# Adding an expert's scaled outputs into the result by accumulating DMAs instead of GpSimd additions

## The chip, the core and the metric

The kernel runs on one core of one Trainium2 chip. The core has TensorE (PE, matrix products into PSUM), VectorE (DVE), ScalarE (ACT), GpSimd (POOL) and SyncE (SP, which here only issues DMAs), each with its own instruction queue, and 16 DMA engines that serve the queues of SP and POOL. The metric is the device time of one execution in microseconds (us); lower is better.

## The reference

A block-sparse attention gives x, and a mixture of eight experts, all of them applied to every token, gives the result. Cut to what matters here:

```python
x = attn_out.transpose(0, 2, 1, 3).reshape(B * S, H * D)     # 3072 tokens x 512
P = exp(x @ w_gate - max); 8 rounds of row and column normalization   # 3072 x 8
out = np.zeros((N, D), dtype=np.float32)
for e in range(E):                       # E = 8, F = 1024
    h = np.maximum(x @ w1[e], 0.0)
    ye = h @ w2[e]
    out += P[:, e:e + 1] * ye
```

## The kernel before

The first part (some 160 us) computes the attention, expert 0 for all tokens and the routing weights `P_sb`. The rest is experts 1 to 7, and the change is in it alone.

Tokens are taken in three pairs of blocks (`p`, 2 x 512 tokens each). Both products of an expert are done by a Strassen scheme in two-by-two blocks with seven products in place of eight. The first layer works in groups of 4 quads per pair of blocks (`quad`, with `product` at L724): seven products of two 512-column matmuls, evicted by ACT and DVE into a ring of `h` tiles (f16), with DVE's `add_relu` (L764) for two of the four blocks. After every second quad DVE forms four sums of `h` blocks (`h_sum`, L776, 128x1024 f16) that the second layer's products need. Weights get such sums too (`w1_sum` L707, `w2_sum` L717).

The second layer works on 4 columns of tokens per pair of blocks (`pair(e, p, c)`, with `project` at L780): seven products of four 256-column matmuls for two tiles of 128 tokens, `t1` and `t2`. The result is kept as float32 in SBUF, `out_acc` (128 x 24 x 512), and each tile gets its parts like this:

- tile t2: DVE multiplies by P and adds from PSUM (`accumulate`, L808) twice, `z1` and `u3`;
- tile t1, first part: the PSUM tile pY holds its left half after product 1, and its right half's share after product 6 in the same columns. ACT copies it, scaled by P, into the two halves of an SBUF tile `y` (`scaled`, L817: `a1`, `a2`). Product 6 (`p6`) waits for `a1`, product 7 for `a2`. GpSimd then adds `y` into `out_acc` (`add_scaled`, L821: `g1`);
- tile t1, second part, in PSUM tile yps: for even c DVE multiplies and adds (`z2`, L808), after `g1`; for odd c ACT scales it into another `y` tile (`a3`) and GpSimd adds it (`z2`, L821), after `g1`. The very last column (e = 7, p = 2, c = 3) goes as an even one.

There are three `y` buffers. In expert 7 SP stores each tile of `out_acc` once `u3` or `z2` is done (L824).

The order on every engine is fixed when the program is built. A planner (`Plan`) holds all pieces of work as units with an engine, a cost in us, predecessors, a priority and the buffers they open or use; `order()` runs a list schedule with these costs and emits the units as it places them. In the hardware each engine then works through its own queue in that order, waiting for semaphores. A buffer tag listed in the planner's slots is a resource: a unit that opens a buffer can be placed only when all users of the buffer it replaces have been placed, and not before they end. The `y` buffers are not among the tags before the change. A unit on an engine name of its own (such as "LAND") models a delay.

Weights for expert e+1 are loaded by POOL's DMA queue (`load_w1` L189, `load_w2` L195), with a cast from float32 to f16, about an expert ahead. POOL has nothing else to do in this part than these loads and the additions.

Of the kernel before, what the change touches and what calls it, by code (L numbers as in the profile page):

```python
# [9 lines left out]
FP32 = mybir.dt.float32  # L10
# [3 lines left out]
ALU = mybir.AluOpType  # L14
# [19 lines left out]
class Plan:  # L34
# [7 lines left out]
    def add(self, eng, cost, fn, deps=(), prio=0.0, opens=(), uses=(), lag=0.0):  # L42
        u = Unit(eng, cost, fn, [d for d in deps if d is not None], prio, list(opens), lag)
        for b in list(opens) + list(uses):
            b.users.append(u)
        if uses and eng != "PE":
            u.prio -= 100.0
        self.units.append(u)
        return u
# [79 lines left out]
def kernel(  # L129
# [10 lines left out]
    nc = tc.nc  # L140
# [3 lines left out]
    N, DM = out.shape  # L144
    E = moe_w_gate.shape[1]
# [33 lines left out]
    out_acc = persist.tile([128, NT, DM], FP32)  # L179
# [40 lines left out]
    NS = 1  # L220
    NA = 3
    stage = ExitStack()
    with tc.manual_schedule():
# [25 lines left out]
        NPAIR = N // (2 * BLK)  # L249
# [1 line left out]
        HK = KD // 2  # L251
        xs, h_ring = {}, {}

        plan = Plan({"m": 3, "s": NS, "a": NA, "A": 3, "R": 1, "Q": 1})
        add = plan.add

        at, units = {}, {}
# [339 lines left out]
        def keep_busy(n):  # L597

            t = bank("m", "idle")
            for _ in range(n):  # L600
# [6 lines left out]
                          in_=k[0, 0:2].rearrange("j (p g) d -> p j (g d)", g=G))  # L607
        nc.sync.dma_start(out=v_f32.rearrange("p j g d -> p (j g) d"),
                          in_=v[0, 0:2].rearrange("j (g p) d -> p (j g) d", p=128))
# [70 lines left out]
        post = {}  # L680
# [99 lines left out]
        def project(e, p, c, n):  # L780
            if n == 1:
                at["ya", e, p, c] = post["ps"].tile([128, BLK], FP32, tag="A", name="pY", bufs=plan.slots["A"])
            elif n == 5:
                at["z", e, p, c] = bank("m", "yps")
            dst = at["ya" if n in (1, 6, 7) else "z", e, p, c]
            d = slice(HD, DM) if n in (5, 3) else slice(0, HD)
            for f in range(HF):
                lhsT = ring(e, p, f)[:, f % 2, {1: 0, 2: 2, 3: 6, 4: 3, 5: 4, 6: 5, 7: 1}[n], c * 128:(c + 1) * 128]
                rhs = {1: lambda: w2s[e][:, f, 0:HD], 2: lambda: w2s[e][:, HF + f, 0:HD],
                       3: lambda: w2s[e][:, HF + f, HD:DM], 4: lambda: at["t", e, 2][:, f, :],  # L790
                       5: lambda: at["t", e, 0][:, f, :], 6: lambda: at["t", e, 1][:, f, :],
                       7: lambda: w2s[e][:, f, HD:DM]}[n]()
                nc.tensor.matmul(dst[:, d], lhsT=lhsT, rhs=rhs, start=f == 0 and n in (1, 5, 2), stop=f == HF - 1,  # L793
                                 skip_group_check=True)

        def tok(p, c, r):
            return 8 * p + 4 * r + c

        def accumulate(e, p, c, r):

            t = tok(p, c, r % 2)
            o, scalar = out_acc[:, t, :], P_sb[:, t, e:e + 1]
            if r == 3:
                o = o.rearrange("p (i d) -> p i d", i=2)
                y = at["ya", e, p, c][:, None, 0:HD].to_broadcast([128, 2, HD])
            else:
                y = at["z", e, p, c][:]
            nc.vector.scalar_tensor_tensor(out=o, in0=y, scalar=scalar, in1=o, op0=ALU.mult, op1=ALU.add)  # L808

        def scaled(e, p, c, part):  # L810

            t, key = tok(p, c, 0), ("y", e, p, c, part == 2)
            if part != 1:
                at[key] = post["sb"].tile([128, DM], FP32, tag="y", name="y", bufs=3)
            d = (slice(0, HD), slice(HD, DM), slice(0, DM))[part]
            src = at["z", e, p, c][:] if part == 2 else at["ya", e, p, c][:, 0:HD]
            nc.scalar.activation(out=at[key][:, d], in_=src, func=AF.Copy, bias=0.0, scale=P_sb[:, t, e:e + 1])  # L817

        def add_scaled(e, p, c, key):
            o = out_acc[:, tok(p, c, 0), :]  # L820
            nc.gpsimd.tensor_tensor(out=o, in0=o, in1=at.pop(("y", e, p, c, key))[:], op=ALU.add)  # L821

        def store(t):
            nc.sync.dma_start(out=out[t * 128:(t + 1) * 128, :], in_=out_acc[:, t, :])  # L824

        def scale_first(eng, t):
            o, scalar = out_acc[:, t, :], P_sb[:, t, 0:1]
            if eng == "ACT":
                nc.scalar.activation(out=o, in_=o, func=AF.Copy, bias=0.0, scale=scalar)
            else:  # L830
                nc.vector.tensor_scalar_mul(out=o, in0=o, scalar1=scalar)
# [201 lines left out]
        for i in range(PB):  # L1033
# [3 lines left out]

        first = {"T": lambda i: U["tr", i, 0], "Q": lambda i: U["tr", i, 1], "k": lambda i: U["kT", i, 0],
                 "q": lambda i: U["kT", i, 1], "v": lambda i: U["vs", i], "V": lambda i: U["Vs", i],
                 "m": lambda i: U["ks", i], "S": lambda i: U["S", i, 0], "X": lambda i: U["X", i, 0],  # L1040
                 "b": lambda i: U["mk", i, 0], "s": lambda i: U["ss", i, 0], "e": lambda i: U["sx", i, 0],
                 "A": lambda i: U["A", i, 0], "n": lambda i: U["no", i, 0], "t": lambda i: U["xt", i, 0],
                 "x": lambda i: U["x", i, 0]}
# [11 lines left out]
        for i in range(PB, NP):  # L1055
# [3 lines left out]
            if i % PB == PB - 1:  # L1059
                b = i // PB  # L1060
# [111 lines left out]
        def pair(e, p, c):  # L1172
            g = (e - 1) * NPAIR + p
            pr = 2005.0 + 10.0 * (HF * (g + 1) + c)
            ya, z = Buffer("A"), Buffer("m")
            t1, t2 = tok(p, c, 0), tok(p, c, 1)
            first = {t1: [], t2: []}
            if e == 1:
                for t in (t1, t2):
                    u = add({"ACT": 0.75, "DVE": 0.5}, 0, None, [U["P"], U["yo", t]], pr - 20.0)  # L1180
                    u.fn = lambda u=u, t=t: scale_first(u.on, t)
                    first[t] = [u]

            def mul(n, deps, opens=False):
                u = add("PE", 0.44, lambda: project(e, p, c, n), deps + [d for j in range(2) for d in U["D", e, p, j][n]],
                        pr, **{"opens" if opens else "uses": [ya if n in (1, 6, 7) else z]})
                U["Yp", e, p, c, n] = u
                return u

            def ev(eng, us, fn, deps, b):  # L1190
                return add(eng, us, fn, deps + [U["P"]], pr - 5.0, uses=[b])

            T = lambda i: U["w2", e, i]
            p1 = mul(1, [U["w2", e]], True)
            a1 = ev("ACT", 0.46, lambda: scaled(e, p, c, 0), [p1], ya)
            p5 = mul(5, [T(0)], True)
            p4 = mul(4, [T(2), p5])
            z1 = ev("DVE", 0.76, lambda: accumulate(e, p, c, 1), [p4] + first[t2], z)
            p6 = mul(6, [T(1), a1])
            a2 = ev("ACT", 0.46, lambda: scaled(e, p, c, 1), [p6], ya)  # L1200
            g1 = add("POOL", 1.25, lambda: add_scaled(e, p, c, False), [a2] + first[t1])
            p3 = mul(3, [z1])
            p7 = mul(7, [T(3), a2])
            u3 = ev("DVE", 0.76, lambda: accumulate(e, p, c, 3), [p7, z1], ya)
            p2 = mul(2, [p3])
            if c % 2 and (e, p, c) != (E - 1, NPAIR - 1, 3):
                a3 = ev("ACT", 0.68, lambda: scaled(e, p, c, 2), [p2], z)
                z2 = add("POOL", 1.25, lambda: add_scaled(e, p, c, True), [a3, g1])
            else:
                z2 = ev("DVE", 0.76, lambda: accumulate(e, p, c, 0), [p2, g1], z)  # L1210
            U["Y", e, p, c] = z2
            if e == E - 1:
                add("SP", 0.1, lambda: store(t2), [u3])
                add("SP", 0.1, lambda: store(t1), [z2])
# [58 lines left out]
```

## Time and profile before

| what | value |
|---|---|
| median of 3 runs | 708.64 us (707.03 to 708.86) |
| the profiled execution's own time | 706.25 us |
| its span, first to last instruction | 704.4 us |
| PE busy | 667.4 us, 95% |
| DVE busy | 611.2 us, 87% |
| ACT busy | 413.0 us, 59% |
| POOL busy | 264.4 us, 38% |
| granted clock of TensorE | 1.000 |

A row of groups reads: line, engine, operation, written tile<-read tiles, shapes and count, then the group's busy time (us), the mean time of one (ns), and the idle time of the engine just before them with what ended most of it. A row of waits reads: who waited, for whom, us in total, how often, the longest. A row of windows reads: the stretch, its length, then busy time and instruction count of each engine (PE, PE's weight loads, DVE, ACT, POOL where all are listed; PE and its weight loads alone where one line of matmuls is asked for), the granted clock, the DMA engines' busy share and GB/s. A row of the timeline reads: start (us), duration (us), engine, line, operation and tiles, how many were merged, and in brackets the idle time before it with what ended it. Matmuls are pipelined and their ends are modelled, so the time between starts says more than their durations.

### The profile page before, as it was taken

Reading aid. Unit: us, or ns where it says so; the run is one execution under the profiler, and the core shown is the slowest. Engines: PE = TensorE matmul, PEld = TensorE weight load, DVE = VectorE, ACT = ScalarE, POOL = GpSimd, SP = SyncE. Lnnn points to the kernel's source line nnn. Section 1 sums busy time; section 2 is a strip of 40 time slices with the busy share of each in tenths; the row PEclk is TensorE's granted clock in tenths of the full one; section 3 lists DMA queues with packets and bytes.
Section 4 is the critical chain, followed back from the end, with each engine's and each line's share of the span. In section 5 each row is a group of like instructions: output and inputs, shape, how many; then the busy total and the mean of one; then the engine's idle time right before and its main releaser. Section 6 shows DMA issues by size and latency. Waiting matters only on the chain.

```text
span 704.4 us, 13246 instructions
## 1 busy us (share of the span) xinstructions
PE 667.4 (95%) x5130; PEld 434.1 (62%) x5131; DVE 611.2 (87%) x1033; ACT 413.0 (59%) x770; POOL 264.4 (38%) x257
## 2 busy tenths in 40 slices
PE   8999999999999999999999999999999899999996
PEld 4666666546666666665666566565666566565665
DVE  7889877999889987989889987989889988989886
ACT  6677765488655556455655546555554655555652
POOL 8899422001323423234324423324323323233224
PEclk9999999999999999999999999999999999999999
DMA  9999924333003030034003120034003210001224
GB/s 170 173 140 146 144 43 79 67 57 65 0 1 61 7 54 1 1 60 61 0 1 61 19 42 1 1 61 60 1 1 60 30 33 1 1 1 46 90 75 150
DMA packets 95262, 36.43 MB, mean 52 GB/s; under 512 B 76000, under 2 KB 88544, under 8 KB 95200
## 3 DMA queue, kind: packets, MB, share of 16 engines
q0 software_dynamic: 77520, 25.99, 34.4%
q1 hardware_dynamic: 17152, 9.58, 5.7%
q8 instruction: 40, 0.66, 0.4%
q14 instruction: 22, 0.18, 0.1%
q10 hardware_dynamic: 528, 0.02, 0.0%
HBM read 52.45 MB, written 6.29 MB: 83 GB/s over the span
## 4 chain that ended last, share of the span: by engine, by line
PE 58%; DVE 28%; issue 7%; DMA 4%; POOL 2%; SPq 0%; DVEq 0%; POOLq 0%
DVE h L776 13%; PE yps L793 13%; PE pA L742 13%; PE pY L793 10%; PE pQ L742 7%; DVE h L764 5%; PE hps L208 4%; PE yps L213 4%; DVE out_acc L808 4%; PE pR L742 3%; DVE w2sum L717 3%; DMA kT<-kst 1%; DMA w<-in_moe_w_dram 1%; DMA vx<-in_v_dram 1%; DMA Ve<-vx 1%
## 5 line engine op out<-in xcount | busy, mean ns | idle before, releaser
L821 POOL TENSOR_TENSOR out_acc<-out_acc,y 128x512 f32<-128x512 f32 x125 | 173.1, 1385 | 366.3 <-ACT y L817 346.3
L793 PEld LDWEIGHTS <-h 128*128 128x128 f16 x2352 | 228.4, 98 | 105.3 <-DVE h L776 13.9
L817 ACT ACTIVATE y<-pY,P_sb 128x256 f32<-128x256 f32 x168 | 79.9, 476 | 144.6 <-PE pY L793 142.8
L776 DVE TENSOR_TENSOR h<-h 128x1024 f16<-128x1024 f16 x168 | 162.2, 998 | 1.4
L808 DVE SCALAR_TENSOR_TENSOR out_acc<-yps,P_sb,out_acc 128x512 f32<-128x512 f32 x127 | 94.1, 742 | 22.0 <-PE yps L793 21.0
L793 PE MATMUL yps<-w2sum,h 128*128 128x256 f16 x672 | 100.3, 273 | 8.2 <-DVE h L776 8.2
L793 PE MATMUL pY<-w,h 128*128 128x256 f16 x672 | 100.3, 272 | 0.1
L742 PE MATMUL pA<-xT,w 128*128 128x512 f16 x336 | 98.4, 379 | 1.6 <-DVE snap L204 1.6
L793 PE MATMUL yps<-w,h 128*128 128x256 f16 x672 | 93.8, 273 | 1.6 <-DVE out_acc L808 1.4
L742 PEld LDWEIGHTS <-w 128*128 128x128 f16 x672 | 65.7, 98 | 41.0 <-issue 10.5
L742 PEld LDWEIGHTS <-w1sum 128*128 128x128 f16 x504 | 49.3, 98 | 60.3 <-issue 18.9
L808 DVE SCALAR_TENSOR_TENSOR out_acc<-pY,P_sb,out_acc 128x512 f32<-128x512 f32 x84 | 62.5, 744 | 20.3 <-PE pY L793 17.4
L764 DVE CUSTOM_DVE_ANT_0 h<-pA,snap 128x512 f16<-128x512 f32 x84 | 57.2, 680 | 6.1 <-PE pA L742 5.7
L199 ACT ACTIVATE h<-pA 128x512 f16<-128x512 f32 x84 | 50.6, 602 | 19.4 <-PE pA L742 19.2
L764 DVE CUSTOM_DVE_ANT_0 h<-pQ,snap 128x512 f16<-128x512 f32 x84 | 57.4, 683 | 5.0 <-ACT snap L204 2.7
L742 PE MATMUL pQ<-xsum,w1sum 128*128 128x512 f16 x168 | 49.9, 378 | 11.1 <-DVE h L764 11.1
L742 PE MATMUL pA<-xsum,w 128*128 128x512 f16 x168 | 49.9, 379 | 5.4 <-DVE h L764 5.3
L199 ACT ACTIVATE h<-pR 128x512 f16<-128x512 f32 x84 | 50.1, 596 | 6.9 <-PE pR L742 6.8
L793 PE MATMUL pY<-w2sum,h 128*128 128x256 f16 x336 | 51.4, 273 | 0.7
L204 ACT COPY snap<-pQ 128x512 f32<-128x512 f32 x70 | 41.0, 586 | 17.1 <-PE pQ L742 17.1
L742 PE MATMUL pA<-xsum,w1sum 128*128 128x512 f16 x168 | 50.0, 379 | 0.0
L742 PE MATMUL pQ<-xT,w1sum 128*128 128x512 f16 x168 | 50.0, 379 | 0.0
(144 smaller groups left out, 860.2 us busy)
## 6 DMA issues: line engine op xcount, KB each, us to landing
w<-in_moe_w_dram POOLq DMA_DIRECT2D x15, 1024.0 KB, 8.8
out_dram<-out_acc SPq DMA_DIRECT2D x24, 256.0 KB, 2.0
qst<-in_q_dram POOLq DMA_DIRECT2D x32, 96.0 KB, 5.7
vx<-in_v_dram POOLq DMA_DIRECT2D x15, 192.0 KB, 6.9
kst<-in_k_dram POOLq DMA_DIRECT2D x24, 96.0 KB, 6.1
w<-in_moe_w_dram POOLq DMA_DIRECT2D x4, 256.0 KB, 7.1
kst<-in_k_dram POOLq DMA_DIRECT2D x3, 192.0 KB, 4.6
Ve<-vx SPq DMA_DIRECT2D x32, 10.2 KB, 5.4
```

The source lines that it names most:

```text
L199: nc.scalar.activation(out=out, in_=in_, func=AF.Relu, bias=0.0, scale=1.0)
L204: (nc.scalar.copy if eng == "ACT" else nc.vector.tensor_copy)(out=out, in_=in_)
L208: nc.tensor.matmul(hp[:, 0:n], lhsT=w1s[e][:, dk, f * 128:(f + 1) * 128], rhs=xT[:, dk, t0:t0 + n], start=(dk == 0), stop=(dk == KD - 1))
L213: nc.tensor.matmul(yp[:, d], lhsT=h[:, f, c * 128:(c + 1) * 128], rhs=w2s[e][:, f, d], start=(f == 0), stop=(f == KF - 1))
L717: nc.vector.tensor_tensor(out=out_, in0=a, in1=b, op=ALU.subtract)
L742: nc.tensor.matmul(dst[:], lhsT=lhsT, rhs=rhs, start=first and k == 0, stop=k == HK - 1, skip_group_check=True)
L764: nc.vector._custom_dve(dve_ops.TENSOR_ADD_SAT, out=ring(e, p, q)[:, q % 2, blk, :], in0=at[src, e, p, q][:], in1=at.pop(("snap", n, e, p, ...
L776: nc.vector.tensor_tensor(out=h[:, :, out_, :], in0=h[:, :, a, :], in1=h[:, :, b, :], op=op)
L793: nc.tensor.matmul(dst[:, d], lhsT=lhsT, rhs=rhs, start=f == 0 and n in (1, 5, 2), stop=f == HF - 1, skip_group_check=True)
L808: nc.vector.scalar_tensor_tensor(out=o, in0=y, scalar=scalar, in1=o, op0=ALU.mult, op1=ALU.add)
L817: nc.scalar.activation(out=at[key][:, d], in_=src, func=AF.Copy, bias=0.0, scale=P_sb[:, t, e:e + 1])
L821: nc.gpsimd.tensor_tensor(out=o, in0=o, in1=at.pop(("y", e, p, c, key))[:], op=ALU.add)
```

## The change

The two GpSimd additions of `pair` become DMAs from the GpSimd queue that read `y` and add it into `out_acc` in SBUF, in float32. The planner gets a unit for the issue on POOL (1.0 us) and one for the landing (4.0 us); the `y` buffers become a planned resource, and there are four of them. In even columns the DVE part now comes first and the DMA of the first part is issued after it; in odd columns the second DMA waits for the landing of the first. In the last pair of blocks of expert 7 the first part stays an addition on GpSimd and the second is a DVE accumulation in every column.

```diff
-        plan = Plan({"m": 3, "s": NS, "a": NA, "A": 3, "R": 1, "Q": 1})
+        plan = Plan({"m": 3, "s": NS, "a": NA, "A": 3, "R": 1, "Q": 1, "y": 4})
...
-                at[key] = post["sb"].tile([128, DM], FP32, tag="y", name="y", bufs=3)
+                at[key] = post["sb"].tile([128, DM], FP32, tag="y", name="y", bufs=plan.slots["y"])
...
         def add_scaled(e, p, c, key):
             o = out_acc[:, tok(p, c, 0), :]
-            nc.gpsimd.tensor_tensor(out=o, in0=o, in1=at.pop(("y", e, p, c, key))[:], op=ALU.add)
+            nc.gpsimd.dma_start(out=o, in_=at.pop(("y", e, p, c, key))[:], accum_op=ALU.add)
+
+        def add_on_pool(e, p, c):
+            o = out_acc[:, tok(p, c, 0), :]
+            nc.gpsimd.tensor_tensor(out=o, in0=o, in1=at.pop(("y", e, p, c, False))[:], op=ALU.add)
...
+            def landed(part, deps, b):
+                u = add("POOL", 1.0, lambda: add_scaled(e, p, c, part == 2), deps)
+                u = add(f"L{e}.{p}.{c}.{part}", 4.0, None, [u])
+                b.users.append(u)
+                return u
+
+            y1 = Buffer("y")
             p1 = mul(1, [U["w2", e]], True)
             a1 = ev("ACT", 0.46, lambda: scaled(e, p, c, 0), [p1], ya)
+            a1.opens.append(y1)
+            y1.users.append(a1)
...
-            g1 = add("POOL", 1.25, lambda: add_scaled(e, p, c, False), [a2] + first[t1])
...
-            if c % 2 and (e, p, c) != (E - 1, NPAIR - 1, 3):
+            last_pair = (e, p) == (E - 1, NPAIR - 1)
+            if c % 2 and not last_pair:
+                g1 = landed(0, [a2] + first[t1], y1)
                 a3 = ev("ACT", 0.68, lambda: scaled(e, p, c, 2), [p2], z)
-                z2 = add("POOL", 1.25, lambda: add_scaled(e, p, c, True), [a3, g1])
+                y2 = Buffer("y")
+                a3.opens.append(y2)
+                y2.users.append(a3)
+                z2 = landed(2, [a3, g1], y2)
+            elif last_pair:
+                g1 = add("POOL", 1.25, lambda: add_on_pool(e, p, c), [a2] + first[t1])
+                y1.users.append(g1)
+                z2 = ev("DVE", 0.76, lambda: accumulate(e, p, c, 0), [p2, g1], z)
             else:
-                z2 = ev("DVE", 0.76, lambda: accumulate(e, p, c, 0), [p2, g1], z)
+                z2 = ev("DVE", 0.76, lambda: accumulate(e, p, c, 0), [p2] + first[t1], z)
+                z2 = landed(0, [a2, z2], y1)
```

## The prediction

> **What bounds the kernel now.** I read the page first, then who waits for whom on PE, then windows that count PE's matmuls, and last the timeline around single idle stretches.
>
> ```profile
> span 704.4 us, 13246 instructions
> L821 POOL TENSOR_TENSOR out_acc<-out_acc,y 128x512 f32<-128x512 f32 x125 | 173.1, 1385 | 366.3 <-ACT y L817 346.3
> L776 DVE TENSOR_TENSOR h<-h 128x1024 f16<-128x1024 f16 x168 | 162.2, 998 | 1.4
> ```
>
> ```profile
> PE pQ L742 <- DVE h L764: 11.1, 26, 0.6
> PE yps L793 <- DVE h L776: 8.2, 12, 0.8
> PE pA L742 <- DVE h L764: 5.3, 6, 0.9
> ```
>
> GpSimd (POOL) is no bound: it idles 366 us ahead of the additions that the change removes. PE bounds, and in experts 1 to 7 nearly all it waits for is VectorE (DVE). PE's shown idle time understates this, since matmul ends are modelled: a product (two 512-column matmuls of L742, or four 256-column ones of L793) shows 0.59 or 0.60 us but the next starts 0.43 us later. So I measure start to start.
>
> ```profile
> 349.77 0.59 PE L742 MATMUL pA<-xT,w 128*128 128x512 f16 x2
> 350.62 0.59 PE L742 MATMUL pQ<-xsum,w1sum 128*128 128x512 f16 x2 [0.26 <-DVE h L764]
> 351.05 0.60 PE L793 MATMUL pY<-w,h 128*128 128x256 f16 x4
> ...
> 362.34 0.59 PE L742 MATMUL pA<-xT,w 128*128 128x512 f16 x2
> 363.20 0.59 PE L742 MATMUL pQ<-xsum,w1sum 128*128 128x512 f16 x2 [0.26 <-DVE h L764]
> ```
>
> From 349.77 to 350.62 is 0.85 us for a 0.43 us product: 0.42 lost, where the row shows 0.26. Then 27 products (350.62 to 362.34, 11.72 us) run at 0.434 us each without a hole, and 0.43 is lost again. With that price the windows give the loss of each stage. The rows count L742, then L793.
>
> ```profile
> 166.80:245.00 78.20, 44.08 (x168) 16.43 (x168) 1.00 0.08 15
> 245.00:638.85 393.85, 221.19 (x840) 82.12 (x840) 1.00 0.16 25
> 638.85:700.40 61.55, 26.36 (x98) 9.58 (x98) 1.00 0.25 95
> ...
> 166.80:245.00 78.20, 45.81 (x350) 33.74 (x349) 1.00 0.08 15
> 245.00:638.85 393.85, 221.91 (x1683) 163.02 (x1681) 1.00 0.16 25
> 638.85:700.40 61.55, 40.32 (x324) 31.39 (x322) 1.00 0.25 95
> ```
>
> The middle stretch is five experts of 78.77 us, each 84 products of L742 and 84 of L793 (the three extra L793 matmuls overlap the edges). 168 x 0.434 = 72.9, so 5.87 us of each expert is lost: 29.3. First stretch: 84 + 87.5 products, 74.4, lost 3.8. Last: 49 + 81, 56.4, lost 5.1. **PE loses 38.2 us in all.**
>
> Who makes DVE late?
>
> ```profile
> 324.37 1.27 POOL L821 TENSOR_TENSOR out_acc<-out_acc,y 128x512 f32<-128x512 f32 x1 [1.45 <-ACT y L817]
> ...
> 324.44 1.74 DVE L776 TENSOR_TENSOR h<-h 128x1024 f16<-128x1024 f16 x1
> ...
> 325.35 0.59 PE L742 MATMUL pA<-xsum,w1sum 128*128 128x512 f16 x2
> 326.84 0.59 PE L742 MATMUL pA<-xsum,w 128*128 128x512 f16 x2 [0.90 <-DVE h L764]
> ```
>
> ```profile
> L776 DVE TENSOR_TENSOR h<-h 128x1024 f16<-128x1024 f16 x157 | 154.0, 1013 | 1.4
> L717 DVE TENSOR_TENSOR w2sum<-w,w2sum 128x1024 f16<-128x1024 f16 x12 | 13.9, 1161 | 0.2
> L707 DVE TENSOR_TENSOR w1sum<-w,w1sum 128x1024 f16<-128x1024 f16 x6 | 10.1, 1683 | 0.0
> L707 DVE TENSOR_TENSOR w<-w 128x1024 f16<-128x1024 f16 x6 | 4.1, 678 | 0.0
> ```
>
> A 128x1024 f16 sum costs 0.68 us alone. One that starts while POOL adds runs 1.74 us and ends 0.54 us after POOL does (326.18 against 325.64): it is held until POOL has read its operands, and loses 1.06 us. PE's hole behind it is 326.84 - 325.35 - 0.43 = 1.06 us, the same number. Over 180 to 700 us these sums lose 157 x 0.335 + 12 x 0.483 + 6 x 1.005 = 64 us of DVE; PE shows 38 of it. Taken from start to start in the same way, one expert's rows show seven holes (1.06, 0.79, 0.42, 0.43, 1.37, 0.79, 0.98), each directly after one or two such sums. The last falls in two, 0.70 of it here (401.43 - 400.51 - 0.22):
>
> ```profile
> 400.51 0.38 PE L793 MATMUL yps<-w2sum,h 128*128 128x256 f16 x2
> 401.43 0.39 PE L793 MATMUL yps<-w2sum,h 128*128 128x256 f16 x2 [0.53 <-DVE h L776]
> ```
>
> The last stage's largest hole is alike:
>
> ```profile
> 685.93 4.83 DVE L776 TENSOR_TENSOR h<-h 128x1024 f16<-128x1024 f16 x4
> ...
> 689.42 0.60 PE L793 MATMUL yps<-w2sum,h 128*128 128x256 f16 x4
> 691.47 1.03 PE L793 MATMUL yps<-w,h 128*128 128x256 f16 x8 [1.44 <-DVE out_acc L808]
> ```
>
> Four sums take 4.83 us where four free ones take about 2.5; PE starts 2.05 us after a 0.44 us product: 1.61 lost.
>
> **The change, part by part.** *Additions removed.* 121 of 125 POOL additions go: 12 + 6 per expert become 120 DMAs, one becomes a DVE addition, and four g1 of the last pair stay. The additions behind all holes but 0.9 us (small ones at 684 and 698 us, where the last pair's additions stay or no sum runs) are among them. Removable: 38.2 - 0.9 = 37.3 us. What is late next is PE itself, at 72.9 us an expert. DVE is busy 347.43 of 393.85 us in the middle stretch (69.5 per expert); less the 64 us (9.8 per expert) it needs 60 of 72.9, 82%.
>
> ```profile
> 245.00:638.85 393.85, 372.13 (x2523) 245.14 (x2521) 347.43 (x461) 220.54 (x420) 132.15 (x98) 1.00 0.16 25
> ```
>
> The granted clock is 1.00 in all these rows, the hole-free stretch among them, so I charge nothing for a denser PE.
>
> *DMAs added: the issue.* POOL now issues 18 DMAs per expert. Does the issue hold the sums as the addition did?
>
> ```profile
> 400.77 0.92 POOL L195 DMA_DIRECT2D w<-in_moe_w_dram  x1
> 401.40 0.69 DVE L776 TENSOR_TENSOR h<-h 128x1024 f16<-128x1024 f16 x1
> ```
>
> This sum ran at 0.69 us with 0.29 us of it inside an issue, so the issue costs it nothing. I take 0, with 0.92 per met sum as the other end. 18 x 0.92 = 17 us of POOL per expert replace 25.
>
> [...]
>
> *The transfer.* 256 KB into SBUF, with the destination read as well: no row shows one.
>
> ```profile
> q0 software_dynamic: 7840, 10.49, 16.7%
> w<-in_moe_w_dram POOLq DMA_DIRECT2D x10, 1024.0 KB, 8.4
> ...
> out_dram<-out_acc SPq DMA_DIRECT2D x24, 256.0 KB, 2.0
> ```
>
> Of the 400 us from 200 to 600, ten weight loads took 16.7% of 16 engines: 6.7 us each for 2 MB read as float32 and 1 MB written. An accumulation reads 512 KB and writes 256 KB, a quarter: 1.7 us. Landing: the plain store takes 2.0; with POOL's issue and a second read I take 3.5 (bounds 2.0 and the weights' 8.4). Engines per expert: 18 x 1.7 + 2 x 6.7 = 44 of 72.9 us, hidden.
>
> [...]
>
> *New waits.* In odd c the second DMA waits on POOL for the first one's landing. Queued behind it are later accumulations and weight loads, which are issued an expert ahead: free. A late landing holds a y buffer, and then ScalarE (ACT), whose first write p6 on PE needs.
>
> ```profile
> 348.12 0.51 ACT L817 ACTIVATE y<-pY,P_sb 128x256 f32<-128x256 f32 x1
> ...
> 353.06 0.75 DVE L808 SCALAR_TENSOR_TENSOR out_acc<-yps,P_sb,out_acc 128x512 f32<-128x512 f32 x1 [0.58 <-PE yps L793]
> ...
> 354.78 0.47 ACT L817 ACTIVATE y<-pY,P_sb 128x256 f32<-128x256 f32 x1 [0.76 <-PE pY L793]
> ```
>
> An even pair's buffer opens at 348.12, its DMA goes after the DVE addition that ends at 353.81, and with 3.5 us it is free some 9 us after opening. Four buffers at three per two pairs (two pairs: 78.77 / 6 = 13.1 us, 12.2 without holes) come round after 16 us. So landings up to about 10 us cost nothing; an accumulation queued behind a whole weight load (6.7 + 3.5) just fits. Bounds 0 to about 2 us, twice per expert; I take 0.
>
> *Moved.* In even c DVE no longer waits for POOL; the last pair's c = 1 gains a DVE addition (0.75 us) and loses an ACT one; stores of expert 7's earlier pairs wait for landings on SP, and the last pair's stores come after them. Nothing. The planner also orders everything anew with the new costs. Bounds: no hole (as in 350.62 to 362.34) to half the old ones; I take a tenth of the 37.3, nearest to the hole-free row.
>
> **Sum.** 37.3 x 0.9 = 33.6 us. The profiled execution took 706.25 us (span 704.4): 672.7. It lies 2.4 below the median of the runs shown (708.64); I say **673**.
>
> **Rivals.**
> [...]
> 2. *The new order makes new waits*, on ACT or a y buffer behind weight loads; half the holes stay: 706.25 - 18.6 = 688. For: ACT already waits for y buffers.
>
> ```profile
> 358.69 0.69 ACT L817 ACTIVATE y<-yps,P_sb 128x512 f32<-128x512 f32 x1 [0.65 <-POOL out_acc L821]
> ```
>
> Against: PE runs on through that wait, and its holes come only behind held sums.
> 3. *Slower: the accumulations fill the DMA engines.* They queue behind each other, y buffers run out, ACT stops, PE stops. Deciding point: 18 t + 13.4 = 78.77, t = 3.6 us of all engines per DMA. If the store's 2.0 us were all transfer and the second read doubled it, t = 4.0: 85.4 an expert, + 6.6 x 6.67 = + 44, **750**. Against: a quarter of a weight load is 1.7.
> 4. *It doesn't do what it says:* the DMAs run, but the sums stay long for another reason, and the time stays. Against: every long sum lies beside a POOL addition.
>
> **How the numbers follow.** Forecast 0.70 (667 to 680), rival 1 0.08, rival 2 0.10, rival 3 0.09, rival 4 0.03. The range, 667.5 to 691, takes in the forecast with all or few holes gone and rivals 1 and 2; 0.12 is left out above. A measurement can tell about 0.3% from no change; faster 0.88, same 0.03, slower 0.09.
>
> **What would show it.** Right: the L776 group's mean falls from 998 to about 680 ns, and matmuls of one stage lie an expert apart at 73 to 74 us, not 78.8; the DMA share rises to about 0.6; PE's waits for L764 and L776 all but vanish. Wrong: long sums beside DMA issues (rival 1), ACT waiting for y on a DMA landing (2), DMA digits at 9 with landings over 10 us (3), a granted clock under 1.00.

## The result, and the profile after

The changed kernel takes 669.85 us (median of 4 runs, 669.34 to 670.20) against 707.84 us before (4 runs, 705.32 to 708.86): a ratio of 0.9468, 95% interval 0.9440 to 0.9496. The profiled execution spans 667.4 us, 37.0 less than the 704.4 before.

The page of the changed kernel, first its busy times, then rows of groups and of DMA issues (tiles, queue, count, size, median us from issue to landing, the moment at which all of its data has arrived):

```profile
span 667.4 us, 13271 instructions
PE 658.2 (99%) x5131; PEld 435.8 (65%) x5131; DVE 547.7 (82%) x1034; ACT 410.0 (61%) x769; POOL 198.2 (30%) x256
...
L821 POOL DMA_DIRECT2D out_acc<-y x120 | 101.3, 879 | 388.1 <-ACT y L817 106.4
L776 DVE TENSOR_TENSOR h<-h 128x1024 f16<-128x1024 f16 x168 | 109.1, 684 | 1.4
...
out_acc<-y POOLq DMA_DIRECT2D x120, 256.0 KB, 3.3
w<-in_moe_w_dram POOLq DMA_DIRECT2D x15, 1024.0 KB, 9.5
```

The sums of h (L776) are the line to look at: the same 168 instructions, 998 ns before, 684 now. The sums of weights that were long before (L717 at 1161 ns, L707 at 1683) take 687 and 681 as well; DVE's other work is as it was: from 160 us on `add_relu` (L764) takes 682 ns before and 685 now, `accumulate` (L808) 743 and 747. PE has gone from 95% to 99%; 120 DMAs stand where the additions stood.

Windows of the stretch of five experts, all engines, and who PE still waits for:

```profile
245.00:609.50 364.50, 364.50 (x2520) 246.49 (x2519) 298.62 (x461) 218.80 (x420) 83.73 (x99) 1.00 0.56 93
```

```profile
PE pY L793 <- ACT y L817: 0.6, 1, 0.6
```

Five experts take 364.5 us, 72.9 each: exactly the 168 x 0.434 of the prediction, with PE busy in all of it and 2520 matmuls = 5 x 504. The DMA engines went from 16% to 56% busy in this stage, and it costs PE nothing. The three rows of PE waiting for L764 and L776 (24.6 us shown) are gone.

### The profile page after: what moved, and what is told of

It reads as the page before. It is cut to its first block, busy times and chain, and to the rows that moved or that the text cites. A ratio compares the mean times of both kernels' runs of the same rounds, so it can differ in the third digit from the quotient of the medians.

```text
span 667.4 us, 13271 instructions
## 1 busy us (share of the span) xinstructions
PE 658.2 (99%) x5131; PEld 435.8 (65%) x5131; DVE 547.7 (82%) x1034; ACT 410.0 (61%) x769; POOL 198.2 (30%) x256
## 4 chain that ended last, share of the span: by engine, by line
PE 94%; DVE 3%; DMA 2%; issue 0%; ACT 0%; SPq 0%; DVEq 0%
PE yps L793 22%; PE pA L742 22%; PE pY L793 17%; PE pQ L742 11%; PE hps L208 5%; PE pR L742 5%; PE yps L213 5%; DMA kT<-kst 1%; PE sg L344 1%; PE av L497 1%; DMA kvf<-in_v_dram 1%; PE vs L352 1%; PE ss L449 1%; PE tx L535 1%; PE tkq L300 1%; PE av L430 1%
## 5 line engine op out<-in xcount | busy, mean ns | idle before, releaser
L821 POOL DMA_DIRECT2D out_acc<-y x120 | 101.3, 879 | 388.1 <-ACT y L817 106.4
L808 DVE SCALAR_TENSOR_TENSOR out_acc<-yps,P_sb,out_acc 128x512 f32<-128x512 f32 x128 | 95.2, 745 | 29.1 <-PE yps L793 29.0
L776 DVE TENSOR_TENSOR h<-h 128x1024 f16<-128x1024 f16 x168 | 109.1, 684 | 1.4
L793 PE MATMUL yps<-w2sum,h 128*128 128x256 f16 x672 | 98.2, 273 | 0.0
L808 DVE SCALAR_TENSOR_TENSOR out_acc<-pY,P_sb,out_acc 128x512 f32<-128x512 f32 x84 | 62.9, 749 | 32.5 <-PE pY L793 31.1
L764 DVE CUSTOM_DVE_ANT_0 h<-pQ,snap 128x512 f16<-128x512 f32 x84 | 57.6, 686 | 5.8 <-ACT snap L204 3.6
L764 DVE CUSTOM_DVE_ANT_0 h<-pA,snap 128x512 f16<-128x512 f32 x84 | 57.5, 684 | 5.7 <-PE pA L742 5.4
L204 ACT COPY pR<-pA 128x512 f32<-128x512 f32 x81 | 46.3, 571 | 6.2 <-PE pA L742 5.4
```

Of the source, the lines that this page charges most:

```text
L204: (nc.scalar.copy if eng == "ACT" else nc.vector.tensor_copy)(out=out, in_=in_)
L764: nc.vector._custom_dve(dve_ops.TENSOR_ADD_SAT, out=ring(e, p, q)[:, q % 2, blk, :], in0=at[src, e, p, q][:], in1=at.pop(("snap", n, e, p, ...
L776: nc.vector.tensor_tensor(out=h[:, :, out_, :], in0=h[:, :, a, :], in1=h[:, :, b, :], op=op)
L821: nc.gpsimd.dma_start(out=o, in_=at.pop(("y", e, p, c, key))[:], accum_op=ALU.add)
```

## The experiments

Each ratio below is to the kernel before, run beside the experiment; a time without a ratio is that of a single run. The theories: **A**: GpSimd additions read SBUF and thereby hold DVE's sums of two SBUF tiles. **B**: the new order made the gain, not the instruction. **C**: the additions cost by being late themselves. **E** and **F** came later, when the DMAs alone turned out slow: **E**, DVE must not wait in its queue for a landing; **F**, the planner must know of landings and buffers. **D**: four buffers are more than is needed.

### The order alone

```diff
         def add_scaled(e, p, c, key):          # changed kernel
-            nc.gpsimd.dma_start(out=o, in_=at.pop(("y", e, p, c, key))[:], accum_op=ALU.add)
+            nc.gpsimd.tensor_tensor(out=o, in0=o, in1=at.pop(("y", e, p, c, key))[:], op=ALU.add)
```

> The changed kernel's plan, order and four y buffers, with GpSimd additions again in place of the accumulating DMAs. Theory A (a GpSimd addition holds DVE's sums of two SBUF tiles): the sums of L776 are long again (mean about 1000 ns in place of 684), PE's holes come back, 695 to 712 us. Theory B (the new order and the freed waits made the gain): sums may be long, but the time stays at 668 to 678 us.

699.56 us, ratio 0.9899 (0.9864 to 0.9934): only 1% faster. Instruction by instruction, PE, ACT and DVE have the same order as in the changed kernel. Its group of sums and PE's waits:

```profile
L776 DVE TENSOR_TENSOR h<-h 128x1024 f16<-128x1024 f16 x168 | 147.4, 910 | 1.4
```

```profile
PE pQ L742 <- DVE h L764: 11.0, 26, 0.6
PE yps L793 <- DVE h L776: 8.5, 12, 0.8
```

With the order held fixed, the instruction is worth 698.0 - 667.4 = 30.6 us of span; the order alone is worth 704.4 - 698.0 = 6.4. The attention part took 1.4 us longer here than in the changed kernel. From the first matmul of expert 1 to the last of expert 7 the three kernels take 549.7, 542.2 and 512.4 us: 7.5 for the order, 29.8 for the instruction, 37.3 in all. Two of the old rows of waits stand as before; the third (pA behind L764, 5.3 us in 6 waits, the 1.06 us hole of the prediction's example) is gone, since in the new order no addition meets that sum: six holes of 1.06 us are 6.3 of the 7.5, and the rest goes with the last pair. A holds, though the mean of 910 ns is under its 1000, and B has a small share of its own, again through the same collision. The split holds for this direction alone; the next run takes the two steps the other way round.

### DMAs alone

```diff
         def add_scaled(e, p, c, key):          # kernel before
-            nc.gpsimd.tensor_tensor(out=o, in0=o, in1=at.pop(("y", e, p, c, key))[:], op=ALU.add)
+            nc.gpsimd.dma_start(out=o, in_=at.pop(("y", e, p, c, key))[:], accum_op=ALU.add)
```

> The kernel before with its plan and order, and only the instruction changed: accumulating DMAs in place of the GpSimd additions. Theory A: sums at 0.68 us; most of the 37 us is gained, less what even columns lose because the DVE addition z2 still waits for g1, now for a landing 3.3 us after the issue, some 0.8 us later than z2 runs now: 670 to 690 us. Theory B: 700 to 712 us.

751.75 us, ratio 1.0636 (1.0609 to 1.0662): neither theory. The sums are at 684 ns, so the collision is gone, and yet the kernel is slower than before by 6%. From the list of waits, then DVE's and PE's timeline beside one weight load, then windows:

```profile
DVE out_acc L808 <- DMA out_acc<-y: 110.0, 38, 7.7
```

```profile
245.58 1.23 POOL L195 DMA_DIRECT2D w<-in_moe_w_dram  x1
248.29 0.84 POOL L821 DMA_DIRECT2D out_acc<-y  x1 [1.48 <-ACT y L817]
```

```profile
249.80 0.75 DVE L808 SCALAR_TENSOR_TENSOR out_acc<-pY,P_sb,out_acc 128x512 f32<-128x512 f32 x1
257.63 0.75 DVE L808 SCALAR_TENSOR_TENSOR out_acc<-yps,P_sb,out_acc 128x512 f32<-128x512 f32 x1 [7.07 <-DMA out_acc<-y]
```

```profile
253.40 0.60 PE L793 MATMUL pY<-w2sum,h 128*128 128x256 f16 x4
259.62 1.01 PE L742 MATMUL pA<-xsum,w 128*128 128x512 f16 x2 [5.62 <-DVE h L764]
```

```profile
252.00:258.40 6.40, 2.00 (x16) 1.37 (x14) 0.77 (x2) 1.44 (x3) 0.84 (x1) 0.88 1.04 164
258.40:264.00 5.60, 4.38 (x18) 2.40 (x18) 3.89 (x7) 0.64 (x2) 0.00 (x0) 0.53 0.02 4
```

In even columns z2 (DVE) still waits for g1, now a landing. The accumulation issued at 248.29 comes 2.7 us after a weight load in the same DMA queue and lands some 9 us later; z2 waits 7.07 us for it, everything behind z2 in DVE's queue waits too, and PE stops for 5.8 us. In the second window the granted clock is 0.53: two 512-column matmuls show 1.01 us where 0.59 is usual. The expectation had priced a landing at 3.3 us with 0.8 us of it late; the mean of the 38 waits is 2.9. Five of them are behind a weight load as here, 7.1 to 7.7 us each and 37 of the 110 us. The other 33, 73 us, are 0.5 to 4.3 us long, most of them for a landing 3.3 to 3.5 us after its issue: the old order puts z2 too soon for any landing.

### A GpSimd instruction that reads, and one that only writes

Both have the changed kernel's DMAs, with three y buffers (the fourth one's place is the scratch tile's).

```diff
...
+            scr = post["sb"].tile([128, DM], FP32, tag="scr", name="scr", bufs=1)
+            nc.gpsimd.tensor_tensor(out=scr[:], in0=y[:], in1=y[:], op=ALU.add)    # first run
...
+            nc.gpsimd.memset(scr[:], 0.0)                                           # second run, twice
```

> The changed kernel (three y buffers) with a GpSimd addition y + y into a scratch tile after every DMA issue; nothing waits for the scratch tile. Theory A: the sums that meet it are held, mean of L776 900 to 1050 ns, holes on PE, 690 to 715 us. Theory C (the additions cost by being late themselves, as writers of out_acc and readers of y): 668 to 676 us with sums at 0.68 us.

> As the run with the scratch additions, but with two GpSimd memsets of the scratch tile, which write and read nothing. Theory A in its narrow form (only reads of GpSimd hold the sums): sums at 0.68 us, 668 to 676 us. In its wide form (any GpSimd instruction on SBUF holds them): sums long where they meet, mean 800 to 1000 ns, 680 to 710 us.

721.69 and 684.73 us. The groups of sums, of the first and the second run, with PE's largest wait in the first and the memsets of the second:

```profile
L776 DVE TENSOR_TENSOR h<-h 128x1024 f16<-128x1024 f16 x168 | 160.3, 988 | 1.3
```

```profile
PE pQ L742 <- DVE h L764: 20.5, 19, 1.8
```

```profile
L776 DVE TENSOR_TENSOR h<-h 128x1024 f16<-128x1024 f16 x168 | 109.1, 684 | 1.3
```

```profile
L824 POOL MEMSET scr<- 128x512 f32 x120 | 100.7, 839 | 0.0
L825 POOL MEMSET scr<- 128x512 f32 x120 | 62.9, 524 | 6.9
```

An addition whose result nobody waits for brings the long sums back, some longer than ever (up to 2.5 us), and PE's waits for them, so C falls. (The buffer y that it reads comes free later, but ACT waits for that once, 0.6 us.) Memsets take 1.4 us beside each DMA and leave the sums at 684 ns, none over 694, so being busy is not enough: the instruction that reads SBUF holds the sums, the one that only writes does not. One that reads and adds nothing was not run. Both times lie above their expectations, some 10 us of it with the three buffers, as the next run shows (680 us). The memset run's other 5 are in the attention part, which took 154.0 us against 150.0; the granted clock was 0.988 over the whole run, against 1.000 with three buffers alone; experts 1 to 7 take 523.1 us, against 522.4 without memsets and 560.4 with the additions.

### Fewer buffers

```diff
-        plan = Plan({..., "y": 4})
+        plan = Plan({..., "y": 3})      # second run: "y": 2
```

> The changed kernel with three y buffers in place of four, in the plan and in SBUF. Theory A with y buffers as a reserve for the landings behind weight loads: three buffers come round in some 12 us, an accumulation behind a weight load holds one for about 15, so ACT waits for y up to 3 us, twice per expert at most, PE stands behind p6: 672 to 690 us, sums at 0.68 us. Theory D (four buffers are more than is needed): 668 to 672 us.

> The changed kernel with two y buffers. Theory A: two buffers come round in 8 us, less than the 9 us for which an even column holds one, so ACT waits in every expert without any weight load: 720 to 800 us, sums at 0.68 us. Theory D: under 690 us.

680.09 us, ratio 0.9611 (0.9582 to 0.9640), and 724.58 us, 1.0251 (1.0200 to 1.0302). Three buffers cost 10 us against four, two cost 55, so D falls. With three, from GpSimd's, ACT's and PE's timeline:

```profile
471.48 1.23 POOL L195 DMA_DIRECT2D w<-in_moe_w_dram  x1
473.14 0.84 POOL L821 DMA_DIRECT2D out_acc<-y  x1 [0.43 <-ACT y L817]
```

```profile
484.78 0.47 ACT L817 ACTIVATE y<-pY,P_sb 128x256 f32<-128x256 f32 x1 [2.81 <-DMA out_acc<-y]
```

```profile
485.30 0.60 PE L793 MATMUL pY<-w2sum,h 128*128 128x256 f16 x4 [1.79 <-ACT y L817]
```

An accumulation is issued 1.66 us after a weight load and lands 11.6 us later; the buffers are all taken, ACT waits 2.81 us, and PE's product 6 behind it 1.79. The changed kernel has the same sequence on GpSimd in each expert, with landings of up to 11.5 us, and four buffers carry it: ACT waits for y on a DMA once in the whole kernel, for 0.3 us.

### More accumulations

After each accumulation, one or two more of the same size add zeros into a tile of `out_acc` that is not in use; three y buffers, so the run above is the base.

```diff
...
+            for r in range(1):       # second run: range(2)
+                nc.gpsimd.dma_start(out=out_acc[:, tok((p + 1) % NPAIR, c, (r + key) % 2), :],
+                                    in_=post["zero"][:], accum_op=ALU.add)
```

> The changed kernel with three y buffers, and after every accumulation a second one of the same size that adds zeros into a tile of out_acc that nobody uses then. With 1.58 us of all engines per accumulation (55.5% of 400 us less ten weight loads of 6.7 us, by 98) the engines have 36 x 1.58 + 13.4 = 70 of 72.9 us of work per expert: close to full, longer landings, ACT waits for y: 675 to 720 us.

> As the run with doubled accumulations, with two extra ones each. The engines then have 54 x 1.58 + 13.4 = 99 us of work per expert against 72.9 for PE: the DMA engines set the pace, + 26 x 6.67 = + 172 us, 800 to 880 us. If accumulations share the engines better than the sum of their busy times tells: under 720 us.

707.89 and 835.03 us, the second near the 667 + 172 = 839 that the sum gives. Queue rows of 200 to 600 us: the changed kernel, doubled, tripled.

```profile
q0 software_dynamic: 22053, 36.39, 55.5%
```

```profile
q0 software_dynamic: 33874, 57.91, 87.8%
```

```profile
q0 software_dynamic: 37765, 65.74, 99.7%
```

The third row is a full queue: the DMA engines set the pace, as rival 3 of the prediction had it, but only at three times the change's traffic. Most of the change's gain is gone well before that: at twice the traffic, 87.8%, landings get long (4.3 us median), ACT waits for y for 39 us in all, and experts 1 to 7 take 544.9 us, against 522.4 for the base and 549.7 for the kernel before.

### Which part of the new order is needed

Three runs. First, the changed kernel with the old sequence in even columns, planned with landings; second, the changed kernel with landings unknown to the plan; third, the kernel before with DMAs and nothing but the new sequence in even columns (three buffers, planned neither as buffers nor as landings).

```diff
-                z2 = ev("DVE", 0.76, lambda: accumulate(e, p, c, 0), [p2] + first[t1], z)   # first run
-                z2 = landed(0, [a2, z2], y1)
+                g1 = landed(0, [a2] + first[t1], y1)
+                z2 = ev("DVE", 0.76, lambda: accumulate(e, p, c, 0), [p2, g1], z)
...
-                u = add(f"L{e}.{p}.{c}.{part}", 4.0, None, [u])                              # second run
+                u = add(f"L{e}.{p}.{c}.{part}", 0.0, None, [u])
...
-            g1 = add("POOL", 1.25, lambda: add_scaled(e, p, c, False), [a2] + first[t1])     # third run
+            if odd:
+                g1 = add("POOL", 1.25, lambda: add_scaled(e, p, c, False), [a2] + first[t1])
...
-                z2 = ev("DVE", 0.76, lambda: accumulate(e, p, c, 0), [p2, g1], z)            # third run
+                z2 = ev("DVE", 0.76, lambda: accumulate(e, p, c, 0), [p2] + first[t1], z)
+                z2 = add("POOL", 1.25, lambda: add_scaled(e, p, c, False), [a2, z2])
```

> The changed kernel with even columns in the old order: the DMA of the first part is issued after a2, and the DVE addition z2 waits for its landing; the plan knows the landing (1 + 4 us). Theory E (DVE waiting in its queue for a landing is what made the run with DMAs alone slow, whatever the plan knows, since a landing behind a weight load takes 10 us and not 5): PE's holes come twice per expert, 680 to 720 us. Theory F (it was slow because the plan did not know of landings): 668 to 678 us. Sums at 0.68 us in both.

> The changed kernel with landings at 0 in place of 4 us in the plan; instructions, waits and the four y buffers are the same, only the order may differ. Theory E (the order of the waits counts, the plan's 4 us do not, since nothing on PE's path waits for a landing with four buffers): 668 to 676 us. Theory F: over 680 us.

> The kernel before with accumulating DMAs, planned as before (three y buffers, not planned; 1.25 us for each), and one more edit: in even columns the DVE addition comes first and the DMA of the first part after it, so that DVE waits for no landing. Theory E (the run with DMAs alone lost its time in DVE's waits for landings): DVE's waits for DMAs vanish, ACT's waits for y behind weight loads stay as with three planned buffers: 675 to 695 us. If the planned buffers and landings are needed as well (theory F): 700 us and more.

684.61 us (ratio 0.9698, 0.9644 to 0.9753), 670.15 us (0.9489, 0.9440 to 0.9539) and 676.43 us (0.9561, 0.9524 to 0.9599). The first one's DVE waits, and PE behind one of them:

```profile
DVE out_acc L808 <- DMA out_acc<-y: 14.6, 6, 3.2
```

```profile
485.95 0.59 PE L742 MATMUL pQ<-xsum,w1sum 128*128 128x512 f16 x2
489.42 1.40 PE L793 MATMUL yps<-w,h 128*128 128x256 f16 x8 [2.87 <-DVE out_acc L808]
```

E and F each hold in part. With the landing in the plan, the old sequence still costs 14 us of span (681.4), nearly all of it in five holes of 2.4 to 3.0 us on PE, one per expert and not two, where DVE waits in its queue for a landing. That is E. The chain of the hole shown starts at an odd column: its first DMA is issued 3.2 us after a weight load, at 473.03, and lands 9.55 us later. GpSimd's queue stands until then, because the column's second DMA waits for it. The even column's DMA behind it is issued at 483.6 and lands at 487.9, and z2 waits for that.

But the run with DMAs alone lies 82 us above the changed kernel, and this one 15, with 23 us of the gain kept: DVE's waits for landings fall from 110.0 us to 14.6, and the 33 shorter ones are gone but for one of 0.9. The plan, which knows the landing, puts z2 later. That is F. The four buffers came with it; they were not run apart, but ACT waited only 6 us for y with DMAs alone.

In the new sequence DVE waits for no landing, and there the planner's 4 us are not needed. The second run loses nothing that can be measured. PE (in experts 1 to 7, up to its last 20 matmuls), ACT and DVE get the same order as in the changed kernel; only GpSimd's differs, with the weight load of w2 some 6 us earlier. The third run, the kernel before with DMAs and that one swap, gets 31 us (707.40 to 676.43) where the whole change gets 38. The third run's span of 672.8 us is 5.4 above the changed kernel's. Its last store waits for a landing, from GpSimd's last rows:

```profile
666.18 0.84 POOL L821 DMA_DIRECT2D out_acc<-y  x1 [1.89 <-issue]
```

In the changed kernel the last addition is DVE's, and DVE ends at 663.7 us; here the last DMA is only issued at 666.2, and the last store at 669.6. From PE's last matmul to the end it takes 8.0 us against 4.5, so some 3.4 of the 5.4 us are this wait; the other 2 are holes on PE, most of them in the last pair. Keeping the last pair on GpSimd and DVE saves both, though it was not run alone. Three unplanned buffers nearly do in the third run: before the last pair PE loses 0.7 us, where three planned ones cost 10. The order on PE is the changed kernel's, and the first accumulation comes 6.2 us after the issue of the load of w2, not 1.7; either may be why (not tried apart). The expectation had ACT wait for y as with three planned buffers, 20.9 us; it waits 6.2.

### What the addition adds to a DMA

```diff
-            nc.gpsimd.dma_start(out=o, in_=at.pop(("y", e, p, c, key))[:], accum_op=ALU.add)
+            nc.gpsimd.dma_start(out=o, in_=at.pop(("y", e, p, c, key))[:])
```

> The changed kernel with plain copies in place of accumulations: the y tile overwrites the tile of out_acc, so that these additions are left out. It measures what the addition adds to a DMA of 256 KB inside SBUF. If the second read costs as much as the first, the engines' time per DMA falls from 1.58 to about 0.8 us and the landing from 3.3 to about 2.7 us; if it costs nothing, both stay. The time stays at 667 to 672 us in both.

671.25 us, without the additions. The landings of the changed kernel's DMAs, and of the copies, with the copies' queue row (200 to 600 us):

```profile
DMA to landing us min/median/max: 3.2/3.3/11.5
```

```profile
DMA to landing us min/median/max: 2.2/2.3/9.7
...
q0 software_dynamic: 15680, 36.18, 33.9%
```

33.9% of 400 us are 135.6. Less ten weight loads at 6.7 us, an estimate from the kernel before, the copies take (135.6 - 67) / 99 = 0.69 us of all engines each, the accumulations (222 - 67) / 98 = 1.58: the addition more than doubles the transfer and adds 1.0 us to the landing. None of it shows in the time.

## Why the prediction was right, step by step

- *PE's lost time.* 38.2 us lost, 37.3 removable: the span fell by 37.0, and experts 1 to 7 by 37.3. The holes left are the two small ones at the start of the last pair and one of 0.7 us behind ACT in it, 1.0 us in all.
- *The cause.* Held sums, shown by taking the instruction alone back in an unchanged order (+30.6 us) and by a reading and a writing GpSimd instruction on whose results nothing waits. Sum by sum it is as clear: before, 71 of the 224 sums of h and of weights were long, each beside an addition, and of the 107 that met no addition none took over 0.69 us. It matters which starts first: the 25 sums that were running when an addition began, and 21 that began within 0.03 us behind it, took 0.67 to 0.69 us; the 71 long ones began 0.05 us or more behind it, took 0.99 to 1.76 us, and each ended 0.55 us after its addition. The prediction gave all 37 to replacing the additions; 6 to 8 of it come from the order, which moved one sum per expert out of an addition's way.
- *The mis-sized term.* A tenth of the holes (3.7 us) was kept back for the new order's own waits. They came to nothing: that is the 3 us between 673 and 669.85.
- *The issue on GpSimd.* Taken at 0, measured at 0: 84 of the 224 sums overlap a DMA issue in the changed kernel, and none of all sums is over 0.694 us. The issues are not slowed either: their median is 0.84 us, beside sums and elsewhere. Rival 1, by which the issue holds the sums as the addition did, does not show: the GpSimd instructions that read SBUF raised the mean of L776 to 998 ns (before) and 988 (scratch additions), while beside DMA issues and memsets it stayed at 684.
- *The transfer.* 1.7 us of engines and 3.5 to landing were taken; 1.58 and 3.3 came out. Landings behind a weight load were put at 10.2; up to 11.5 came out, while the weight loads' own landings went from 8.4 to 10.1 us.
- *The buffers.* That landings of about 10 us cost nothing with four held, with little to spare: three planned ones cost 10 us, 9 of it in six holes on PE behind ACT. Rival 2 stood one buffer away, in that order of work.
- *GpSimd's wait in odd columns.* It was put at nothing, and in the changed kernel it costs nothing: GpSimd stands 18 us in all for landings, and nothing on PE's path waits for it. With the old sequence the same wait starts the five holes.
- *DVE's wait in even columns.* "DVE no longer waits for POOL" was entered as moved work worth nothing. Without it the DMAs alone lose 45 us, and the changed kernel, whose plan knows the landings, would gain 23 in place of 38. The prediction counted it right, since the changed kernel has no such wait, but did not see what it was worth; that the change had this step in it was the design's merit and not the forecast's.
- *Slower by full DMA engines.* The way of reckoning holds (835 us measured and 839 reckoned at three times the traffic, from the 1.58 us measured by then); its condition was far off, at 56% busy.

## What to carry to other kernels

When an engine's instruction shows two clusters of durations (the sums of before: 0.67 to 0.69 us, and 0.99 to 1.76), look at what runs beside the long ones before blaming its own work: 1.06 us lost by a sum was, to the hundredth, the hole on PE. Moving the additions to DMAs paid most here where DVE waits for no landing: 38 us gained with the DMA placed after DVE's own addition, 23 with it before. Where an engine must wait, tell the plan of the landing, and count the one behind the longest transfer of the same queue (up to 11.5 us here, not 3.3). The last pieces before the end were better kept on an engine here: from PE's last matmul to the end it took 4.5 us with them there, 8.0 with a landing to wait for.

## What the runs showed of the hardware that was not expected

- One changed instruction made the kernel 6% slower, although it did away with every collision (sums at 684 ns); a DVE queue that waits for a DMA behind a 1 MB load stands for up to 7.7 us.
- After a hole on PE the granted clock can be at half. With DMAs alone PE stood from 253.83 to 259.62 us, and the clock was 0.53 from 258.40 to 264.00 us and 1.00 in the 11 us that follow; over the whole execution it was 0.968. In the run with the old sequence a hole of 3.04 us, from 486.38 us, was followed by the 4 us below, at 0.59: from 490.61 to 493.17 us PE's products start 0.85 to 0.86 us apart in place of 0.434. Over that whole execution the clock was 0.997, which is about 4 us at half speed (an estimate, 0.003 x 681.4 / 0.5), so little more than this one stretch for its five holes of 2.4 to 3.0 us. With three buffers no fall followed the hole of 1.96 us from 483.34 us: the next product starts 0.44 us after the one that ended it, and the clock was 1.000 over the execution. What decides it was not shown.

```profile
489.20:493.20 4.00, 3.78 (x15) 1.87 (x15) 3.41 (x6) 1.87 (x3) 0.84 (x1) 0.59 0.02 2
```

- An accumulating DMA takes GpSimd 0.84 us to issue, two thirds of the 1.27 us of the addition that it replaces; it is the reading of SBUF and not GpSimd's time that mattered (the memsets keep it busy for 1.36 us beside each issue and leave the sums at 684 ns).
